# Preparing batch 2 of a linear-attention and token-mixer kernel earlier: phi of q and its transpose one block sooner, kv to mm1 four to five slots sooner, two relus on VectorE

## The chip, the cores and the metric

The kernel runs on one core of a Trainium2 chip. The metric is the device time of one execution in microseconds (us), lower is better. Times of one kernel are given as the median of several runs. Traces come from the hardware profiler; times inside a trace count from the start of its span, which is some 1.8 us shorter than the device time. In the profile lines PE is TensorE, PEld its weight loads, DVE VectorE, ACT ScalarE, POOL GpSimd and SP SyncE; L169 is line 169 of the kernel. PSUM is the memory into which TensorE writes; the granted clock is the share of full speed that TensorE was given.

## The reference

Eight batches of 576 tokens. A linear attention with eight heads of 64 feeds a mixer layer that mixes first over tokens (through 256) and then over channels (512 to 1536 and back).

```python
def phi(x):
    return np.where(x > 0, x, np.exp(x) - 1.0) + 1.0
q_p, k_p = phi(q), phi(k)
kv  = np.einsum('bhsd,bhse->bhde', k_p, v)
z   = np.sum(k_p, axis=2)
num = np.einsum('bhsd,bhde->bhse', q_p, kv)
den = np.einsum('bhsd,bhd->bhs', q_p, z)[..., None] + 1e-06
x   = (num / den)                      # heads side by side: (batch, 576, 512)
h   = np.maximum(x.T @ w_tok1, 0) @ w_tok2        # per batch
u   = x + h.T
out = u + np.maximum(u @ w_ch1, 0) @ w_ch2
```

## The kernel before

The schedule is written by hand. Each batch has a front part (phi, `kv`, `nd` = num/den, `mm1` and `mm2` over tokens) and a heavy part (`mm3` and `mm4` over channels). A block runs the heavy part of one batch as a list `big` of pieces, and after piece number s it emits whatever `fill` holds for slot s: the front part of the next batch and the loads of a later one. Each engine takes its instructions in the order in which they were emitted, so a slot is a place in five queues at once. "mm3 number 8" is the piece mm3(1, 8), and "relu 8" the relu behind it.

```python
def phi_exp(nm, n, j0, nj):            # ScalarE
    nc.scalar.activation(out=e, in_=f, func=AF.Exp)
def phi_add(nm, n, j0, nj):            # VectorE
    nc.vector.tensor_scalar(out=y, in0=f, scalar1=1.0, ..., op0=ALU.add)
def phi_end(nm, n, j0, nj):            # VectorE: max(min(e, 1), y)
    nc.vector.tensor_scalar(out=e, in0=e, scalar1=1.0, ..., op0=ALU.min)
    nc.vector.tensor_tensor(out=dst..., in0=e..., in1=y..., op=ALU.max)
def phi(nm, n, c):
    phi_exp(nm, n, 2*c, 2); phi_add(nm, n, 2*c, 2); phi_end(nm, n, 2*c, 2)

def vcast(n, c, copy=nc.scalar.copy):  # v to bf16; half 0 on ScalarE, half 1 on VectorE
    ...
def qtr_dma(n):                        # transpose of phi(q), two DMAs from SyncE's queue
    for a in range(2):
        nc.sync.dma_start_transpose(out=qT[n % 2]..., in_=qp[half[a]]...)

def nd(n, g, rs):                      # 2 or 4 matmuls, then VectorE: den, 1/den, x = num/den
    nd_mm(n, g, rs); nd_end(n, g, rs)
def mm1(n):                            # 10 matmuls; number 5 and 10 need the x of nd20 and nd21
    ...                                # then two relus on ScalarE into ar

def mm3(n, mc, kjs=range(NDM), dve=False):     # 4 matmuls into one of four PSUM buffers
    ...
    if dve: nc.vector.tensor_scalar(out=cr..., in0=ps, scalar1=0.0, ..., op0=ALU.max)
    else:   nc.scalar.activation(out=cr..., in_=ps, func=AF.Relu)

# block 0 (batch 0's mm3 and mm4, with the front part of batch 1), cut
big = [... 12 x mm3(0, mc) ..., 12 x m4_0(kc)]
at0 = {"kv": 14, "nd00": 15, ..., "nd20": 19, "nd21": 20, "mm1": 21}
fill += [(23, fn) for fn in (mm4_end(0, 0), mm4_end(0, 1), mm2_half(1, 0), ...)]
# block 1 (batch 1's mm3, tails, mm4, with the front part of batch 2)
big = [mm3(1, mc, second halves) for mc in 0, 1, 2] + m3(1, 3) + m3t + m4(0, [4, 5, 6, 7, 8])
at1 = {"kv": 11, "nd00": 13, ..., "nd21": 18, "mm1": 20, "mm2a": 21, "mm2b": 22, "mm2t": 24, ...}
fill = phi("q", 2, 0 / 1) at 0, 2; qtr_dma(2) and load_all(3) at 3; phi("k", 2, 0 / 1) at 4, 6;
       vcast(2, 0) at 8, vcast(2, 1, VectorE) at 9; phi("q", 3) at 19, 23; ...
```

Of the kernel before, what the change touches and what calls it, by code (L numbers as in the profile page):

```python
# [18 lines left out]
def kernel(  # L19
# [20 lines left out]
    nc = tc.nc  # L40
# [13 lines left out]
    NCH = DCH // 128  # L54
# [54 lines left out]
    def load(nm, n, c, gate=None):  # L109
        src_ = src[nm][n].rearrange("(j a) (p t) d -> (a p) j (t d)", a=2, t=T)  # L110
        js = slice(2 * c, 2 * c + 2)
        return after(nc.sync.dma_start(out=raw[nm, n % 2][:, js], in_=src_[:, js]), gate)
# [9 lines left out]
    def phi_exp(nm, n, j0, nj):  # L122
        f = raw[nm, n % 2][:, j0:j0 + nj].rearrange("p j f -> p (j f)")
        e = work.tile([128, 2 * TD], BF16, name="e", tag="e", bufs=4)[:, :nj * TD]
        nc.scalar.activation(out=e, in_=f, func=AF.Exp)  # L125
        live["e", j0] = e

    def phi_add(nm, n, j0, nj):
        f = raw[nm, n % 2][:, j0:j0 + nj].rearrange("p j f -> p (j f)")
        y = work.tile([128, 2 * TD], BF16, name="y", tag="y", bufs=1)[:, :nj * TD]  # L130
        nc.vector.tensor_scalar(out=y, in0=f, scalar1=1.0, scalar2=None, op0=ALU.add)  # L131
        for j in range(nj):
            live["y", j0 + j] = y[:, j * TD:]

    def phi_end(nm, n, j0, nj):
        c, i = divmod(j0, 2)
        dst = (kp if nm == "k" else qp)[:, c, :, i:i + nj]
        e, y = live["e", j0], live["y", j0][:, :nj * TD]
        nc.vector.tensor_scalar(out=e, in0=e, scalar1=1.0, scalar2=None, op0=ALU.min)  # L139
        nc.vector.tensor_tensor(  # L140
            out=dst.transpose([0, 2, 1, 3]), in0=e.rearrange("p (i t d) -> p i t d", i=nj, t=T),
            in1=y.rearrange("p (i t d) -> p i t d", i=nj, t=T), op=ALU.max)

    def phi(nm, n, c):
        phi_exp(nm, n, 2 * c, 2)
        phi_add(nm, n, 2 * c, 2)
        phi_end(nm, n, 2 * c, 2)

    def vcast(n, c, copy=nc.scalar.copy):
        js = slice(2 * c, 2 * c + 2)  # L150
        copy(out=vs[:, js, :, 0:D],  # L151
             in_=raw["v", n % 2][:, js].rearrange("p j (t d) -> p j t d", t=T))
# [9 lines left out]
    def kv(n, cs):  # L162
        b = n % 2
        ps = ps_sm.tile([128, 2, 512], FP32, name="kv_ps", tag="sm")[:, :, 0:2 * D1].rearrange(
            "p a (c e) -> p a c e", c=2)
        for c in cs:
            for t in range(T):
                for a, i in QUARTERS:
                    nc.tensor.matmul(out=ps[half[i], a, c], lhsT=kp[half[a], c, t, i],  # L169
                                     rhs=vs[half[a], 2 * c + i, t],  # L170
                                     start=(t == 0), stop=(t == T - 1))
        cs = slice(cs[0], cs[-1] + 1)
        for i in range(2):
            at = slice(i * D1, (i + 1) * D1)
            nc.scalar.copy(out=kvbd[b][half[i], cs, :, at].transpose([0, 2, 1, 3]),
                           in_=ps[half[i], :, cs])
# [13 lines left out]
    def qtr(n, c, put=nc.scalar.copy):  # L190
        tp = ps_sm.tile([128, 2, 8, 128], BF16, name="tp", tag="sm")
        for h, ts in enumerate(TS):
            qtr_mm(c, ts, tp[:, h])
        for h, ts in enumerate(TS):
            qtr_put(n, c, ts, tp[:, h], put)

    def qtr_dma(n):
        for a in range(2):
            nc.sync.dma_start_transpose(
                out=qT[n % 2][:, 2 * TD * a:2 * TD * (a + 1)].rearrange("p (f s) -> p f s", s=D),  # L200
                in_=qp[half[a]].rearrange("p c t i d -> p (c t i d)"))
# [26 lines left out]
    def nd(n, g, rs):  # L228
        nd_mm(n, g, rs)
        nd_end(n, g, rs)  # L230
# [215 lines left out]
    def w2_put(kt):  # L446
        nc.scalar.copy(out=w2p[:, TD * kt:TD * (kt + 1)].rearrange("k (t p) -> k t p", t=T),
                       in_=w2r[:, kt].transpose([0, 2, 1]))
# [8 lines left out]
    def utr_dma(n, rs):  # L457
        b = n % 2
        nc.sync.dma_start_transpose(
            out=uT[b][:, rs[0]:rs[0] + len(rs)].rearrange("p r j c -> p (r j) c"),  # L460
            in_=u[b][:, rs[0]:rs[0] + len(rs)].rearrange("p r d -> p (r d)"))
# [7 lines left out]
    def mm3(n, mc, kjs=range(NDM), dve=False):  # L469
        b = n % 2  # L470
        if kjs[0] == 0:
            part_of[mc] = ps_big.tile([128, 512], FP32, name="c_ps", tag="big")
        ps = part_of[mc]
        for kj in kjs:
            nc.tensor.matmul(out=ps, lhsT=wc1[:, kj, 128 * mc:128 * mc + 128],  # L475
                             rhs=uT[b][:, :, kj],
                             start=(kj == 0), stop=(kj == NDM - 1))
        if kjs[-1] == NDM - 1 and dve:
            nc.vector.tensor_scalar(out=cr[b][:, mc, :], in0=ps, scalar1=0.0, scalar2=None,
                                    op0=ALU.max)  # L480
        elif kjs[-1] == NDM - 1:
            nc.scalar.activation(out=cr[b][:, mc, :], in_=ps, func=AF.Relu)  # L482
# [49 lines left out]
    def prep_k(n, g, copy=nc.scalar.copy):  # L532
        phi("k", n, g)
        vcast(n, g, copy)

    def load_all(n, nms):
        if n < B:
            for nm in nms:
                for g in range(2):
                    load(nm, n, g)  # L540
# [51 lines left out]
    dve, act = nc.vector.tensor_copy, nc.scalar.copy  # L592
# [57 lines left out]
    def steps(n):  # L650

        out_ = [("kv", lambda: kv(n, range(2)))]
        if n == 1:
            puts = [nc.scalar.copy, nc.vector.tensor_copy if n == 1 else nc.scalar.copy]
            out_ += [(f"qt{c}", lambda c=c: qtr(n, c, puts[c])) for c in range(2)]
        for i, rs in enumerate(([0, 1], [2, 3], [4])):
            for g in range(2):
                out_.append((f"nd{i}{g}", lambda g=g, rs=rs: nd(n, g, rs)))
        out_.append(("mm1", lambda: mm1(n)))
        if n > 1:  # L660
            out_ += [("mm2a", lambda: mm2(n, [0, 1])), ("mm2b", lambda: mm2(n, [2, 3])),
                     ("mm2t", lambda: mm2(n, [R]))]
            out_ += [("uta", lambda: utr_dma(n, [0, 1])), ("utb", lambda: utr_dma(n, [2, 3]))]
            if n % 2:
                out_.append(("utt", lambda: utr_tail_dma(n // 2)))
        return out_

    def run(bigs, fill):
# [5 lines left out]
        for s, fn in fill:  # L674
            assert s < len(bigs)

    m3 = lambda n, k0=0: [lambda mc=mc: mm3(n, mc) for mc in range(k0, NCH)]
    m3t = [lambda i=i: mm3_tail(i) for i in range(3)]
    m4 = lambda p, ts: [lambda t=t, i=i: mm4(p, t, range(4 * i, 4 * i + 4))
                        for t in ts for i in range(3)]  # L680
# [6 lines left out]
    big = [lambda mc=mc: mm3(0, mc, range(2, 4)) for mc in range(3)] + \  # L687
# [4 lines left out]
    fill = [(2, mm2_first_tail)]  # L692
# [4 lines left out]
                 (en, lambda nm=nm, c=c: phi_end(nm, 1, 2 * c, 2))]  # L697
    late = [("vc", lambda: vcast(1, 0)), ("vc", lambda: vcast(1, 1, nc.vector.tensor_copy))]
    fill += [(16 + kt, lambda kt=kt: w2_put(kt)) for kt in range(NT)]
    first = steps(1)  # L700
    for nm, fn in first[1:3] + late + first[0:1] + first[3:]:
        fill += [(at0[nm], fn)]
# [7 lines left out]
    for mc in range(3):  # L710
        mm3(1, mc, range(0, 2))
    utr_tail(0)
    big = [lambda mc=mc: mm3(1, mc, range(2, 4)) for mc in range(3)] + m3(1, 3) + m3t + m4(0, [4, 5, 6, 7, 8])
    at1 = {"kv": 11, "nd00": 13, "nd01": 14, "nd10": 15, "nd11": 16, "nd20": 17, "nd21": 18,
           "mm1": 20, "mm2a": 21, "mm2b": 22, "mm2t": 24, "uta": 21, "utb": 22}
    fill = [(s, lambda g=g: phi("q", 2, g)) for g, s in ((0, 0), (1, 2))]
    fill += [(3, lambda: qtr_dma(2)), (3, lambda: load_all(3, "qkv"))]
    fill += [(s, lambda g=g: phi("k", 2, g)) for g, s in ((0, 4), (1, 6))]
    fill += [(8, lambda: vcast(2, 0)), (9, lambda: vcast(2, 1, nc.vector.tensor_copy))]
    fill += [(at1[nm], fn) for nm, fn in steps(2)]  # L720
    fill += [(s, lambda g=g: phi("q", 3, g)) for g, s in ((0, 19), (1, 23))]
    fill += [(24, lambda: qtr_dma(3)), (24, lambda: load_all(4, "qkv"))]
    fill += [(s, lambda g=g: prep_k(3, g)) for g, s in ((0, 25), (1, 27))]
    run(big, sorted(fill, key=lambda e: e[0]))

    AT3 = {"kv": 1, "nd00": 3, "nd01": 4, "nd10": 5, "nd11": 6, "nd20": 7, "nd21": 8,
# [3 lines left out]
    for n in range(2, B):  # L730
        p, b = divmod(n, 2)
        if b == 0:
            big = m3(n) + m4(p, [0, 1, 2, 3])
        else:
            big = m3(n) + m3t + m4(p, [4, 5, 6, 7, 8] if n + 1 < B else [8, 4, 5, 6, 7])
        fill = []
# [40 lines left out]
```

## Time and profile before

| | before |
|---|---|
| time, median of 3 runs | 268.45 us (267.95 to 268.59) |
| span of the profiled run | 266.5 us |
| TensorE / VectorE / ScalarE busy | 96% / 59% / 50% |

The prediction below shows the page's first part, the stretch of mm3 in block 1 and the end of block 0. The timeline of TensorE of the kernel before, later in block 1 and at the start of block 2 (start, duration, engine, line, operation, tiles, count):

```profile
79.88 1.28 PE L261 MATMUL h_ps<-ar,w2p 128*128 128x512 bf16 x4
81.00 1.02 PE L501 MATMUL h_ps<-wc,cr 128*128 128x512 bf16 x4
81.86 1.03 PE L261 MATMUL h_ps<-ar,w2p 128*128 128x512 bf16 x4
...
91.02 1.07 PE L169 MATMUL kv_ps<-vs,kp 64*64 64x65 bf16 x72
```

Four such matmuls without a hole are recorded with 1.03 us; the first group has 1.28. That is how a short hole shows: no idle time is listed, the group is only longer. And the list of what TensorE waited for, in the kernel before (total, times, longest):

```profile
PE kv_ps L169 <- ACT vs L151: 0.5, 1, 0.5
...
PE nd_ps L210 <- DMA qT<-qp: 0.3, 1, 0.3
```

The first is batch 2's kv at 67.1 us; the second is batch 4's nd at 120.4, far behind the change.

### The profile page before, as it was taken

Reading aid. Unit: us, or ns where it says so; the run is one execution under the profiler, and the core shown is the slowest. Engines: PE = TensorE matmul, PEld = TensorE weight load, DVE = VectorE, ACT = ScalarE, POOL = GpSimd, SP = SyncE. Lnnn points to the kernel's source line nnn. Section 1 sums busy time; section 2 is a strip of 40 time slices with the busy share of each in tenths; the row PEclk is TensorE's granted clock in tenths of the full one; section 3 lists DMA queues with packets and bytes.
Section 4 is the critical chain, followed back from the end, with each engine's and each line's share of the span. In section 5 each row is a group of like instructions: output and inputs, shape, how many; then the busy total and the mean of one; then the engine's idle time right before and its main releaser. Section 6 shows DMA issues by size and latency. Waiting matters only on the chain.

```text
span 266.5 us, 5141 instructions
## 1 busy us (share of the span) xinstructions
PE 256.1 (96%) x2107; PEld 133.9 (50%) x2107; DVE 157.4 (59%) x309; ACT 132.9 (50%) x202; POOL 32.6 (12%) x54
## 2 busy tenths in 40 slices
PE   7899989999999999999999999999999999999992
PEld 3684445553744454445564554445564554444641
DVE  5864967469587876947684296938684272420121
ACT  5735764269718368525771358425870353036300
POOL 9710200110000300030001300030001300000000
PEclk9999999999999999999999999999999999999999
DMA  7999999353957695799999990671066500730043
GB/s 259 248 203 282 367 197 398 138 132 97 345 200 156 151 387 204 87 210 373 323 410 225 287 391 9 143 164 41 2 130 120 118 2 0 157 99 2 0 118 79
DMA packets 49927, 48.34 MB, mean 181 GB/s; under 512 B 30256, under 2 KB 35248, under 8 KB 49904
## 3 DMA queue, kind: packets, MB, share of 16 engines
q1 hardware_dynamic: 41824, 35.53, 45.1%
q0 software_dynamic: 7440, 11.44, 20.3%
q10 hardware_dynamic: 640, 1.05, 1.2%
q8 instruction: 16, 0.26, 0.4%
q14 instruction: 7, 0.06, 0.1%
HBM read 35.85 MB, written 9.44 MB: 170 GB/s over the span
## 4 chain that ended last, share of the span: by engine, by line
PE 78%; DVE 7%; DMA 5%; ACT 4%; issue 2%; POOL 1%; ACTq 0%; POOLq 0%
PE h_ps L501 31%; PE c_ps L475 23%; PE a_ps L248 6%; PE h_ps L261 5%; PE c_ps L489 4%; PE nd_ps L210 3%; DMA qT<-qp 3%; DMA cr<-in_v_dram 3%; DVE y L131 2%; PE kv_ps L169 1%; ACT cr L482 1%; ACT e L125 1%; DVE e L139 1%; DVE kp L140 1%; PE bank L363 1%
## 5 line engine op out<-in xcount | busy, mean ns | idle before, releaser
L475 PE MATMUL c_ps<-uT,wc 128*128 128x512 bf16 x384 | 91.3, 379 | 0.7 <-ACT uT L444 0.4
L482 ACT ACTIVATE cr<-c_ps 128x512 bf16<-128x512 f32 x93 | 54.4, 603 | 74.6 <-PE c_ps L475 74.4
L501 PE MATMUL h_ps<-wc,cr 128*128 128x512 bf16 x384 | 87.9, 379 | 0.0
L501 PEld LDWEIGHTS <-cr 128*128 128x128 bf16 x384 | 37.0, 98 | 42.1
L475 PEld LDWEIGHTS <-wc 128*128 128x128 bf16 x384 | 35.9, 98 | 37.7 <-issue 1.8
L518 DVE TENSOR_TENSOR o_sb<-h_ps,u 128x512 f32<-128x512 f32 x32 | 21.8, 688 | 27.3 <-PE h_ps L501 27.2
L523 POOL DMA_DIRECT2D out_dram<-o_sb x24 | 14.4, 606 | 155.1 <-DVE o_sb L518 155.1
L222 DVE TENSOR_TENSOR x<-nd_ps,den 128x512 bf16<-128x512 f32 (+1 forms) x42 | 25.3, 602 | 1.5
L139 DVE TENSOR_SCALAR e<-e 128x1152 bf16<-128x1152 bf16 x30 | 13.9, 463 | 12.4 <-ACT e L125 12.3
L125 ACT ACTIVATE e<-k_raw 128x1152 bf16<-128x1152 f32 x16 | 18.8, 1174 | 2.3 <-DMA k_raw<-in_k_dram 2.3
L273 DVE TENSOR_TENSOR u<-h_ps,x 128x1024 bf16<-128x1024 f32 x12 | 14.3, 1219 | 8.8 <-PE h_ps L261 8.8
L125 ACT ACTIVATE e<-q_raw 128x1152 bf16<-128x1152 f32 x16 | 18.6, 1162 | 1.1 <-DMA q_raw<-in_q_dram 1.1
L219 DVE TENSOR_SCALAR den<-nd_ps 128x8 f32<-128x8 f32 (+1 forms) x42 | 6.8, 163 | 19.7 <-PE nd_ps L210 19.2
L251 ACT ACTIVATE ar<-a_ps 128x512 bf16<-128x512 f32 x14 | 7.6, 595 | 18.1 <-PE a_ps L248 18.1
L210 PEld LDWEIGHTS <-qT 128*128 128x128 bf16 x140 | 11.4, 98 | 10.0 <-DMA qT<-qp 0.6
L261 PE MATMUL h_ps<-ar,w2p 128*128 128x512 bf16 x60 | 16.0, 379 | 0.1
L210 PE MATMUL nd_ps<-kvbd,qT 128*128 128x130 bf16 x140 | 15.3, 223 | 0.3 <-DMA qT<-qp 0.3
L248 PE MATMUL a_ps<-x,w 128*128 128x512 bf16 x56 | 14.4, 379 | 0.0
L151 ACT CAST vs<-v_raw 128x1152 bf16<-128x1152 f32 x12 | 14.0, 1163 | 0.0
L528 DVE TENSOR_TENSOR o_sb<-h_ps,ut 128x512 f32<-128x512 f32 x4 | 2.8, 690 | 18.7 <-PE h_ps L501 18.7
L131 DVE TENSOR_SCALAR y<-q_raw 128x1152 bf16<-128x1152 f32 x16 | 12.4, 775 | 0.3
L140 DVE TENSOR_TENSOR qp<-e,y 128x1152 bf16<-128x1152 bf16 x16 | 12.1, 759 | 0.6
(102 smaller groups left out, 215.4 us busy)
## 6 DMA issues: line engine op xcount, KB each, us to landing
k_raw<-in_k_dram SPq DMA_DIRECT2D x16, 576.0 KB, 8.6
q_raw<-in_q_dram SPq DMA_DIRECT2D x16, 576.0 KB, 7.2
v_raw<-in_v_dram SPq DMA_DIRECT2D x14, 576.0 KB, 10.4
out_dram<-o_sb POOLq DMA_DIRECT2D x24, 256.0 KB, 3.8
wc<-in_moe_w_ch_dram POOLq DMA_DIRECT2D x8, 384.0 KB, 9.8
out_dram<-o_sb SPq DMA_DIRECT2D x10, 128.0 KB, 2.3
out_dram<-o_sb ACTq DMA_DIRECT2D x8, 128.0 KB, 2.6
out_dram<-o_sb POOLq DMA_DIRECT2D x6, 128.0 KB, 7.3
```

What stands on the lines that cost most here:

```text
L125: nc.scalar.activation(out=e, in_=f, func=AF.Exp)
L131: nc.vector.tensor_scalar(out=y, in0=f, scalar1=1.0, scalar2=None, op0=ALU.add)
L139: nc.vector.tensor_scalar(out=e, in0=e, scalar1=1.0, scalar2=None, op0=ALU.min)
L140: nc.vector.tensor_tensor(out=dst.transpose([0, 2, 1, 3]), in0=e.rearrange("p (i t d) -> p i t d", i=nj, t=T), in1=y.rearrange("p (i t d) ...
L210: nc.tensor.matmul(out=o[:, a], lhsT=qT[b][:, t0:t0 + 128], rhs=kvbd[b][:, c, a], start=True, stop=True)
L222: nc.vector.tensor_tensor(out=x[b][:, rs[0]:rs[0] + m, HG * D * g:HG * D * (g + 1)].rearrange("p r (h d) -> p r h d", h=HG), in0=v_[:, :, ...
L248: nc.tensor.matmul(out=ps[:, mt], lhsT=w1t[:, b, ms] if r == R else w1[:, r, ms], rhs=x[b][:, r, :], start=(r == 0), stop=(r == R))
L261: nc.tensor.matmul(out=ps[:, i], lhsT=w2v(kt, r, b), rhs=ar[b][:, kt, :], start=(kt == 0), stop=(kt == NT - 1 and not add))
L475: nc.tensor.matmul(out=ps, lhsT=wc1[:, kj, 128 * mc:128 * mc + 128], rhs=uT[b][:, :, kj], start=(kj == 0), stop=(kj == NDM - 1))
L482: nc.scalar.activation(out=cr[b][:, mc, :], in_=ps, func=AF.Relu)
L501: nc.tensor.matmul(out=ps, lhsT=crt[:, kc, :] if t == 8 else cr[b][:, kc, 128 * r:128 * r + 128], rhs=wc2[:, kc, :], start=(kc == 0), stop ...
L518: nc.vector.tensor_tensor(out=o, in0=ps, in1=u[b][:, r, :], op=ALU.add)
```

## The change

The intent: in block 1, ScalarE does twelve relus, four exps and a cast of batch 2 while TensorE does mm3, and falls behind. So the phi of batch 2's q, its transpose and the next loads go to the end of block 0, where ScalarE idles; the rest of batch 2's front part moves four or five slots up; two relus go to VectorE; and the preparation of batch 3 moves one or two slots up.

```diff
@@ block 0 @@
+    fill += [(20 + g, lambda g=g: phi("q", 2, g)) for g in range(2)]
+    fill += [(22, lambda: qtr_dma(2)), (22, lambda: load_all(3, "qkv"))]
@@ block 1 (lines shortened) @@
-    big = [...] + m3(1, 3) + m3t + m4(0, [4, 5, 6, 7, 8])
-    at1 = {"kv": 11, "nd00": 13, ... "nd21": 18, "mm1": 20, "mm2a": 21, "mm2b": 22, "mm2t": 24, "uta": 21, "utb": 22}
-    fill = [(s, lambda g=g: phi("q", 2, g)) for g, s in ((0, 0), (1, 2))]
-    fill += [(3, lambda: qtr_dma(2)), (3, lambda: load_all(3, "qkv"))]
-    fill += [(s, lambda g=g: phi("k", 2, g)) for g, s in ((0, 4), (1, 6))]
-    fill += [(8, lambda: vcast(2, 0)), (9, lambda: vcast(2, 1, nc.vector.tensor_copy))]
+    big = [...] + [lambda mc=mc: mm3(1, mc, dve=mc in (4, 7)) for mc in range(3, NCH)] + m3t + m4(0, [4, 5, 6, 7, 8])
+    at1 = {"kv": 7, "nd00": 8, ... "nd21": 13, "mm1": 15, "mm2a": 17, "mm2b": 18, "mm2t": 20, "uta": 17, "utb": 18}
+    fill = [(s, lambda g=g: phi("k", 2, g)) for g, s in ((0, 0), (1, 2))]
+    fill += [(4, lambda: vcast(2, 0)), (5, lambda: vcast(2, 1, nc.vector.tensor_copy))]
-    phi("q", 3) at 19, 23; qtr_dma(3), load_all(4) at 24; prep_k(3) at 25, 27
+    phi("q", 3) at 19, 21; qtr_dma(3), load_all(4) at 22; prep_k(3) at 24, 26
```

More of the change, by code (lines that the diff above doesn't have):

```diff
@@ L712 @@
     utr_tail(0)
-    big = [lambda mc=mc: mm3(1, mc, range(2, 4)) for mc in range(3)] + m3(1, 3) + m3t + m4(0, [4, 5, 6, 7, 8])
-    at1 = {"kv": 11, "nd00": 13, "nd01": 14, "nd10": 15, "nd11": 16, "nd20": 17, "nd21": 18,
-           "mm1": 20, "mm2a": 21, "mm2b": 22, "mm2t": 24, "uta": 21, "utb": 22}
-    fill = [(s, lambda g=g: phi("q", 2, g)) for g, s in ((0, 0), (1, 2))]
-    fill += [(3, lambda: qtr_dma(2)), (3, lambda: load_all(3, "qkv"))]
-    fill += [(s, lambda g=g: phi("k", 2, g)) for g, s in ((0, 4), (1, 6))]
-    fill += [(8, lambda: vcast(2, 0)), (9, lambda: vcast(2, 1, nc.vector.tensor_copy))]
+    big = [lambda mc=mc: mm3(1, mc, range(2, 4)) for mc in range(3)] + [lambda mc=mc: mm3(1, mc, dve=mc in (4, 7)) for mc in range(3, NCH)] + m3t + m4(0, [4, 5, 6, 7, 8])
+    at1 = {"kv": 7, "nd00": 8, "nd01": 9, "nd10": 10, "nd11": 11, "nd20": 12, "nd21": 13,
+           "mm1": 15, "mm2a": 17, "mm2b": 18, "mm2t": 20, "uta": 17, "utb": 18}
+    fill = [(s, lambda g=g: phi("k", 2, g)) for g, s in ((0, 0), (1, 2))]
+    fill += [(4, lambda: vcast(2, 0)), (5, lambda: vcast(2, 1, nc.vector.tensor_copy))]
     fill += [(at1[nm], fn) for nm, fn in steps(2)]
-    fill += [(s, lambda g=g: phi("q", 3, g)) for g, s in ((0, 19), (1, 23))]
-    fill += [(24, lambda: qtr_dma(3)), (24, lambda: load_all(4, "qkv"))]
-    fill += [(s, lambda g=g: prep_k(3, g)) for g, s in ((0, 25), (1, 27))]
+    fill += [(s, lambda g=g: phi("q", 3, g)) for g, s in ((0, 19), (1, 21))]
+    fill += [(22, lambda: qtr_dma(3)), (22, lambda: load_all(4, "qkv"))]
+    fill += [(s, lambda g=g: prep_k(3, g)) for g, s in ((0, 24), (1, 26))]
     run(big, sorted(fill, key=lambda e: e[0]))
```

## The prediction

> **What bounds the kernel now.** I read the page's first part, then the timeline of TensorE, then those of ScalarE and VectorE around each hole in it. The first part of the page:
>
> ```profile
> PE 256.1 (96%) x2107; PEld 133.9 (50%) x2107; DVE 157.4 (59%) x309; ACT 132.9 (50%) x202; POOL 32.6 (12%) x54
> PEclk9999999999999999999999999999999999999999
> ```
>
> TensorE is busy 256.1 of 266.5 us at the full clock; the others have room. The change neither adds nor removes a matmul, so it can win or lose only holes in TensorE's stream. The busy figure hides part of them: a 128x512 matmul is recorded with 379 ns, while four back to back take 0.86 us on the chain of waits, 0.216 each. So I look for starts more than 0.216 us apart. In the stretch that the change touches (46 to 92 us) they lie in batch 1's mm3, whose relus share ScalarE with the preparation of batch 2. The timeline there, all engines (start, duration, engine, line, operation, count, idle time before and its releaser):
>
> ```profile
> 56.62 9.97 PE L475 MATMUL c_ps<-uT,wc 128*128 128x512 bf16 x42
> 57.31 0.60 ACT L482 ACTIVATE cr<-c_ps 128x512 bf16<-128x512 f32 x1
> 57.80 1.17 ACT L125 ACTIVATE e<-q_raw 128x1152 bf16<-128x1152 f32 x1
> 58.85 1.09 ACT L482 ACTIVATE cr<-c_ps 128x512 bf16<-128x512 f32 x2
> 59.80 1.18 ACT L125 ACTIVATE e<-q_raw 128x1152 bf16<-128x1152 f32 x1
> 60.85 1.10 ACT L482 ACTIVATE cr<-c_ps 128x512 bf16<-128x512 f32 x2
> 61.51 0.76 DVE L140 TENSOR_TENSOR qp<-e,y 128x1152 bf16<-128x1152 bf16 x1
> ...
> 65.82 1.23 ACT L151 CAST vs<-v_raw 128x1152 bf16<-128x1152 f32 x1
> 66.24 0.76 DVE L151 CAST vs<-v_raw 128x1152 bf16<-128x1152 f32 x1
> ...
> 67.11 0.77 PE L169 MATMUL kv_ps<-vs,kp 64*64 64x65 bf16 x72 [0.51 <-ACT vs L151]
> ```
>
> ScalarE has no idle note from 57.31 on: relu, exp, two relus, exp, and so on. From 56.62 to kv's first matmul at 67.11 there are 10.49 us for 42 matmuls, which need 42 x 0.216 = 9.07. Entering kv costs 0.09 everywhere (116.52 to 117.47 us for four matmuls in the next block), so **1.33 us are stalls**: 0.15, 0.30 and 0.30 where a PSUM buffer (four of them) is still with a late relu, and 0.58 where kv waits for the cast of v. Two more lie later: four mm2 matmuls at 79.88 recorded with 1.28 instead of 1.03 us (0.26, the second half of `ar` not yet out), and batch 3's kv at 91.02 with 1.07 instead of 0.77 (0.29, for kp). The whole prize is 1.33 + 0.26 + 0.29 = 1.9 us, 0.7%.
>
> **What the Trainium skill says.** "Perfetto Trace Analysis", Identifying the Most-Contended Engine: matmul occupancy is no good measure of headroom. The trace agrees (379 ns recorded, 216 apart). "TensorE: Matmul & The Clock Gate", Step-by-step: matmuls stay in program order, only weight loads are pulled ahead. The trace agrees: while kv stands at 66.5 to 67.1, the ready mm3_tail behind it does not run. "PSUM — Partial Sum Buffer", Engine vs sequencer instructions: the queues of ScalarE and VectorE are strict FIFO. It agrees: at 57.2 VectorE idles 1.8 us for one exp. "VectorE: DVE Perf Modes", The perf-mode tier table: PSUM operands keep an operation from the fast modes. It agrees in direction: 463 ns for 128x1152 of SBUF, 675 ns for the smaller 128x512 relu from PSUM.
>
> **The change part by part.**
>
> *1. phi of q of batch 2 goes into batch 0's block (slots 20, 21).* Data: q's two halves are issued at 37.25 and 37.7 us and the trace gives 6.0 and 6.8 us to landing: 43.25 and 44.5. ScalarE is free then:
>
> ```profile
> 49.21 1.08 ACT L251 ACTIVATE ar<-a_ps 128x512 bf16<-128x512 f32 x2 [6.35 <-PE a_ps L248]
> ```
>
> so two exps of 1.17 run at about 43.3 and 44.5 for nothing. VectorE is the trouble. The order of its instructions in the changed program is: nd20's three, the first phi's three, nd21's three, the second phi's three, o_sb. Before:
>
> ```profile
> 45.67 0.42 DVE L222 TENSOR_TENSOR x<-nd_ps,den 128x256 bf16<-128x256 f32 x1
> 46.19 0.16 DVE L219 TENSOR_SCALAR den<-nd_ps 128x4 f32<-128x4 f32 x1
> 46.39 0.18 DVE L221 RECIPROCAL den<-den 128x4 f32<-128x4 f32 x1
> 46.60 0.42 DVE L222 TENSOR_TENSOR x<-nd_ps,den 128x256 bf16<-128x256 f32 x1
> 50.29 1.29 DVE L518 TENSOR_TENSOR o_sb<-h_ps,u 128x512 f32<-128x512 f32 x2 [3.27 <-PE h_ps L501]
> ```
>
> and on TensorE:
>
> ```profile
> 46.85 1.03 PE L248 MATMUL a_ps<-x,w 128*128 128x512 bf16 x4
> 47.72 0.38 PE L248 MATMUL a_ps<-x,w1t 128*128 128x512 bf16 x1
> ```
>
> mm1's fifth matmul, at 47.72, needs nd21's x, ready at 47.02. One phi between others takes 1.83 us from its start to the next one's (76.49 to 78.32). With it at 46.01, nd21's den starts at 47.84, its x at 48.25, done 48.67, and the fifth matmul goes at about 48.73: **+1.0 us**, and mm1 and all behind it shift. The second phi runs 48.6 to 50.4 beside mm1 and ends before o_sb's new time (51.3): free. A hole of 3.27 us was there for both, but the first was put ahead of the instruction that TensorE waits for.
>
> *2. Transpose and loads of batch 3 sooner.* The two transposes (some 4 us each to land) start about 50.5 instead of 62.4; nothing waited for them before. Worth 0.
>
> *3. Block 1 without the q work; kv at slot 7, two relus on VectorE.* Times as before, without the 1.0. ScalarE: relu0 57.31, exp k 57.80, relu1 58.85, relu2 59.35, exp k 59.80, relu3 60.85, v cast 61.35 to 62.55. The sequence up to relu3 is unchanged, so mm3 number 7 still waits 0.15 for its buffer, and the last matmul before kv goes at 62.17. VectorE: the k phis sit where the q phis sat, the second ends at 62.27; then relu4 (0.67), then its v cast 62.95 to 63.7. kv needs ScalarE's cast (62.55, 0.14 late) and, for its second half, VectorE's (63.7, when TensorE would be there at about 62.9): mm3 number 8 starts near 64.18 where 63.03 would be free: stalls 1.15. nd00 follows one slot after kv instead of two, and the kvbd copies (0.76) end at 65.08: 0.1 more. Together 1.25 against 1.33: **-0.1**. The relus after that keep up (ScalarE's five exps and casts in this stretch became three).
>
> *4. Later slots.* mm2a now comes two slots after mm1 instead of one: -0.26. The k phis of batch 3 start a slot sooner and VectorE, back to back from 82.9 to 92 us before, has the q phi behind it sooner: -0.29.
>
> Sum: +1.0 - 0.1 - 0.26 - 0.29 = +0.35, so 268.45 + 0.35 = **268.8 us**.
>
> **The rivals.** *It works as meant*: the early phi costs nothing and kv stops waiting: -1.9, 266.5 us. For it: the holes are real, ScalarE's load falls. Against it: the strict order on VectorE twice, at nd21 and at the cast behind relu4. If nd21's wait alone fails to appear: 267.8. *Late data*: q lands under about 400 GB/s of traffic; e is needed at 46.7 and its exp ends at 44.5, so 2.2 us of slack; landing 3 us late would add about 1 us: 269.8, and ScalarE's relu of mm1 would sit behind the exps. *Collisions*: batch 3's loads run with the output stores instead of after them; both were hidden, and batch 4's transpose (0.3 us of waiting at 120.4) may move either way: +-0.3. In none does another engine become the bound.
>
> **Range and chances.** Three runs before spread over 0.6 us; the hand schedule may be off by 0.5 at each of two places; hence 267.8 to 269.7. Being faster by 2% needs 5.4 us, nearly three times all the holes there are; being slower by 2% needs five such waits as I found.
>
> **What would show it.** In the changed profile: (1) a hole of about 1 us inside mm1 of batch 1 near 48 us, released by VectorE's x; without it I am 1 us too high. (2) kv of batch 2 split by a wait of about 0.7 us for the cast of v on VectorE. (3) the four mm2 matmuls at 1.03 us and batch 3's kv at 0.77. (4) the q transposes issued near 50 us with no waiter. I'd be wrong most if the q data land late, or if a new hole opens after 92 us.

## The result and the profile after

| | before | after |
|---|---|---|
| time, median of 4 runs each | 268.40 us (267.95 to 268.59) | 268.61 us (268.28 to 269.13) |
| span of the profiled run | 266.5 us | 266.8 us |
| granted clock, profiled run | 1.0 | 0.998 |

The ratio after to before is 1.0012, with a 95% interval of 0.9991 to 1.0032: the same. Ratios here are the mean time of one kernel's runs over the mean of the other's runs of the same rounds, so they are not quite the ratio of the medians. Executions over 1.5% slower than the fastest of the same kernel are left out of the means.

The end of block 0 in the changed kernel, timeline of VectorE, ScalarE and TensorE (as above; in brackets the idle time before, and what ended it):

```profile
43.18 2.25 ACT L125 ACTIVATE e<-q_raw 128x1152 bf16<-128x1152 f32 x2
...
46.41 0.75 DVE L131 TENSOR_SCALAR y<-q_raw 128x1152 bf16<-128x1152 f32 x1
...
47.26 0.81 PE L248 MATMUL a_ps<-x,w 128*128 128x512 bf16 x3
47.57 0.76 DVE L140 TENSOR_TENSOR qp<-e,y 128x1152 bf16<-128x1152 bf16 x1
48.25 0.15 DVE L219 TENSOR_SCALAR den<-nd_ps 128x4 f32<-128x4 f32 x1
...
48.65 0.42 DVE L222 TENSOR_TENSOR x<-nd_ps,den 128x256 bf16<-128x256 f32 x1
...
49.13 0.38 PE L248 MATMUL a_ps<-x,w1t 128*128 128x512 bf16 x1 [1.06 <-DVE x L222]
```

The exps are done long before they are needed. One whole phi (46.41 to 48.25, 1.84 us) stands before nd21's den, and mm1's fifth matmul, due at 48.12 us (0.86 us behind the first, at 47.26), runs at 49.13: a hole of 1.01 us. (The trace lacks the record of the fourth, so the list shows 1.06.)

Block 1, the same view:

```profile
62.92 0.76 DVE L140 TENSOR_TENSOR kp<-e,y 128x1152 bf16<-128x1152 bf16 x1
63.59 0.68 DVE L479 TENSOR_SCALAR cr<-c_ps 128x512 bf16<-128x512 f32 x1
...
63.97 0.48 PE L169 MATMUL kv_ps<-vs,kp 64*64 64x65 bf16 x36
64.20 0.75 DVE L151 CAST vs<-v_raw 128x1152 bf16<-128x1152 f32 x1
...
65.00 0.48 PE L169 MATMUL kv_ps<-vs,kp 64*64 64x65 bf16 x36 [0.54 <-DVE vs L151]
```

kv's 72 matmuls are cut in two: the second half waits for VectorE's cast of v, which stands behind relu 4 (line 479). Later, mm2's first matmuls, batch 3's kv and batch 4's first nd:

```profile
77.55 1.03 PE L261 MATMUL h_ps<-ar,w2p 128*128 128x512 bf16 x4
...
91.89 0.78 PE L169 MATMUL kv_ps<-vs,kp 64*64 64x65 bf16 x72
...
120.50 0.54 PE L210 MATMUL nd_ps<-kvbd,qT 128*128 128x130 bf16 x4
```

And the list of TensorE's waits:

```profile
PE a_ps L248 <- DVE x L222: 1.1, 1, 1.1
PE kv_ps L169 <- DVE vs L151: 0.8, 2, 0.5
```

kv's wait for ScalarE has become one for VectorE, a new wait of 1.1 us is there, and batch 4's wait for qT has left the list. It is not quite gone: the four nd matmuls at 120.50 are recorded with 0.54 us where others have 0.40, so 0.14 of its 0.44 us remain.

**A ledger of the trace.** Every run's code is the same up to 40 us, and yet batch 1's kv started anywhere between 38.36 and 39.08 us in the thirteen profiles. To keep this out, I set the start of that kv as zero in each trace and list how far a run is behind (+) or ahead (-) of the kernel before at later landmarks on TensorE:

| us against before | batch 1's tail transposes (before: 56.4) | kv of batch 3 (91.0) | kv of batch 4 (117.5) | kv of batch 5 (150.2) and the end |
|---|---|---|---|---|
| after | +1.01 | +0.47 | +0.18 | -0.01 |

So block 0 lost 1.01, block 1 won 0.54 (1.01 to 0.47), batch 3's kv 0.29, and a further 0.19 came in block 3. Net nothing, with one trace of each; the timed runs say +0.1%, with zero inside the interval.

### The profile page after: what moved, and what is told of

It reads as the page before. It is cut to its first block, busy times and chain, and to the rows that moved or that the text cites. A ratio compares the mean times of both kernels' runs of the same rounds, so it can differ in the third digit from the quotient of the medians.

```text
span 266.8 us, 5122 instructions
## 1 busy us (share of the span) xinstructions
PE 255.8 (96%) x2088; PEld 134.1 (50%) x2107; DVE 158.2 (59%) x311; ACT 132.6 (50%) x200; POOL 33.4 (13%) x54
## 4 chain that ended last, share of the span: by engine, by line
PE 89%; DVE 6%; ACT 2%; issue 1%; POOL 0%; POOLq 0%; ACTq 0%
PE h_ps L501 33%; PE c_ps L475 29%; PE a_ps L248 5%; PE h_ps L261 5%; PE c_ps L489 4%; PE bank L545 3%; PE nd_ps L210 3%; PE kv_ps L169 2%; DVE x L222 1%; ACT e L125 1%; PE bank L363 1%; PE bank L413 1%; DVE y L131 1%; DVE vs L151 1%; PE bank L385 1%
## 5 line engine op out<-in xcount | busy, mean ns | idle before, releaser
L482 ACT ACTIVATE cr<-c_ps 128x512 bf16<-128x512 f32 x91 | 53.5, 598 | 79.0 <-PE c_ps L475 78.9
L501 PE MATMUL h_ps<-wc,cr 128*128 128x512 bf16 x376 | 86.9, 379 | 0.5
```

Of the source, the lines that this page charges most:

```text
L482: nc.scalar.activation(out=cr[b][:, mc, :], in_=ps, func=AF.Relu)
L501: nc.tensor.matmul(out=ps, lhsT=crt[:, kc, :] if t == 8 else cr[b][:, kc, 128 * r:128 * r + 128], rhs=wc2[:, kc, :], start=(kc == 0), stop ...
```

## The experiments

My theory: the changed kernel's time is the sum of a hole made by the order of VectorE's queue at nd21 (+1.0), a hole moved from ScalarE's cast of v to VectorE's, and two mended later holes. Rivals: it is the price of doing q early at all (ScalarE, late data); or the engines are full in this stretch and no order helps. All experiments gave correct results. Each was timed in three or five rounds beside the kernel before. Below, a kernel is called faster or slower only where the interval excludes 1. "Ledger" is the last column of the table above: the trace's end against the kernel before, from batch 1's kv on.

### Both phis ahead of nd21

```diff
-    fill += [(20 + g, lambda g=g: phi("q", 2, g)) for g in range(2)]
+    fill += [(20, lambda g=g: phi("q", 2, g)) for g in range(2)]
```

> The suspected cost doubled: both phis of q ahead of nd21 on VectorE. My theory: mm1's hole grows by one phi, 1.83 us, from 1.0 to 2.85 us, and nothing takes it back: 270.4 us. Rival (the hole is not VectorE's order but the arrival of q or ScalarE): it stays at 1.0, 268.6.

Measured: 271.83 us, ratio 1.0119 (1.0092 to 1.0146); ledger +2.0. The timeline of TensorE:

```profile
51.12 0.38 PE L248 MATMUL a_ps<-x,w1t 128*128 128x512 bf16 x1 [3.01 <-DVE x L222]
```

The wait grows from 1.06 to 3.01 us, by 1.95: one more phi (two in a row are 1.94 apart, start to start, in this trace). The size of the hole is set by what stands ahead of nd21. The median is 3.2 us above the changed kernel's where the profiled spans differ by 2.1 (268.9 to 266.8); the profiled run was the fastest of its six (270.68). The clock may explain that further 1 us of the other five: four of them have a mean granted clock of 0.990 to 0.996, the profiled run 0.999, and two traces further down show slow matmuls behind a long hole. No trace of those five is kept, so it isn't shown.

### Both phis behind nd21, a slot later

```diff
-    fill += [(20 + g, lambda g=g: phi("q", 2, g)) for g in range(2)]
+    fill += [(21 + g, lambda g=g: phi("q", 2, g)) for g in range(2)]
```

> The changed kernel with both early phis of q one slot later, so that VectorE's program has nd21's three instructions ahead of the first phi. My theory (the 1 us hole in mm1 of batch 1 is nd21's x standing behind a 1.83 us phi on VectorE): the hole goes, x is ready as in the kernel before, the two phis fill VectorE's 3.27 us hole and delay the first o_sb by some 0.3 us, which mm2_half hides. 267.6 us, 0.8 to 1.0 below the changed kernel. Rival (the hole is the price of putting ScalarE's exps or q's late data there, whatever the order): the hole stays or moves to mm2_half, 268.4 or more.

Measured: 268.74 us, ratio 1.0012 (0.9989 to 1.0036); ledger +0.5. My number missed. The hole in mm1 is gone, as the theory says, but the timeline shows another one in mm2_half:

```profile
50.82 1.17 ACT L125 ACTIVATE e<-q_raw 128x1152 bf16<-128x1152 f32 x1
...
52.02 0.46 DVE L139 TENSOR_SCALAR e<-e 128x1152 bf16<-128x1152 bf16 x1 [1.74 <-ACT e L125]
...
54.36 0.60 PE L288 MATMUL h_ps<-ar,w2p 128*128 128x256 bf16 x4 [0.67 <-ACT u L291]
```

My edit was careless: at slot 22 the second exp is emitted after mm1's two relus, and ScalarE takes it only when those have waited for mm1. VectorE then stands 1.74 us for it, and its o_sb and u come late. The hole in mm2_half has a second part that I had not thought of: PSUM buffers are assigned when the kernel is built, and in the compiled order of this build the matmul at 54.36 waits for ScalarE, where in the kernel before and in the changed kernel the same one waits for VectorE. So it got another buffer, one that ScalarE frees only at 54.31. The rival is not refuted by this run.

### Exps early, VectorE's part behind nd21

```diff
-    fill += [(20 + g, lambda g=g: phi("q", 2, g)) for g in range(2)]
+    fill += [(20, lambda g=g: phi_exp("q", 2, 2 * g, 2)) for g in range(2)]
+    for g in range(2):
+        fill += [(21, lambda g=g: phi_add("q", 2, 2 * g, 2)), (21, lambda g=g: phi_end("q", 2, 2 * g, 2))]
```

> A repaired version of the run with the phis behind: that run put the second exp of q behind mm1's two relus on ScalarE's queue, so VectorE stood 1.74 us for it and the hole moved into mm2_half. Here both exps stay at slot 20 (ScalarE, idle there), and only VectorE's six instructions go behind nd21's three. Everything else is the changed kernel. My theory: mm1's hole (1.06) goes and none comes in mm2_half, since the two phis end at about the time of the first o_sb; stalls in the trace between 46 and 57 us fall by 0.9 to 1.0, and the time is 0.9 below the changed kernel: about 267.6. Rival (the phis just don't fit into VectorE's 3.27 us hole): 0.5 us or more of new waits in mm2_half, at most 0.5 gained.

Measured: 267.70 us, ratio 0.9978 (0.9949 to 1.0007; one of six runs at 269.52); ledger at the tail transposes 0.00 instead of +1.01, at the end -1.3. Neither mm1 nor mm2_half has a hole that the kernel before doesn't have. So q can be prepared at the end of block 0 for nothing; only the order of VectorE's queue costs 1.0 us. The rival falls. (That rests on the trace: the timed interval still includes 1. 0.45 of the 1.3 come only after 117.5 us, 0.44 of it from batch 4's wait for qT, which this profile lacks.)

### The first part of the change alone

Block 0 as in the changed kernel; block 1's slots and relus as before, less the q work.

```diff
-    (block 1 of the changed kernel)
+    big = ... + m3(1, 3) + m3t + m4(0, [4, 5, 6, 7, 8]); "kv": 11, "nd00": 13, ... as before
+    fill = [(s, lambda g=g: phi("k", 2, g)) for g, s in ((0, 4), (1, 6))]   # no phi of q, no qtr_dma(2), no load_all(3)
```

> Only the first part of the change: phi of q, its transpose and the loads in batch 0's block; block 1 as in the kernel before (kv at 11, all relus on ScalarE). My theory: +1.0 for nd21's x, and -1.3 because ScalarE, without the two exps of q, keeps up with the relus and kv no longer waits; the waits of mm2a (0.26) and of batch 3's kv (0.29) stay. About 268.1 us, 0.3 below the kernel before. Rival (it is kv at slot 7 and the two relus on VectorE that mend block 1): block 1's stalls stay, 269.4.

Measured: 268.23 us, ratio 0.9989 (0.9965 to 1.0013); ledger +1.00 at the tail transposes, -0.32 at batch 3's kv, -0.5 at the end. The timeline of TensorE in block 1:

```profile
58.13 9.23 PE L475 MATMUL c_ps<-uT,wc 128*128 128x512 bf16 x42
67.29 0.78 PE L169 MATMUL kv_ps<-vs,kp 64*64 64x65 bf16 x72
```

42 matmuls in 9.23 us are 42 x 0.216 and the last one's tail (379 ns recorded, 0.216 apart: 0.16): **no stall at all**, against 1.33 us before. Taking the phi of q out of block 1 (two exps off ScalarE, six instructions off VectorE) mends it completely. That kv moved to slot 7 and that two relus moved to VectorE had no part in it; with them, 1.03 us of stalls came back (0.15 for a PSUM buffer, 0.82 before and in kv, 0.06 at nd00).

### The two relus back on ScalarE

```diff
-    ... [lambda mc=mc: mm3(1, mc, dve=mc in (4, 7)) for mc in range(3, NCH)] + m3t ...
+    ... m3(1, 3) + m3t ...
```

> The changed kernel with the two relus of batch 1 back on ScalarE. My theory: they are worth nothing where they stand, for relu4 delays VectorE's cast of v by 0.67 us just before kv needs it. Without it, kv's second half no longer waits (0.54), but ScalarE's cast comes 0.5 later behind relu4 and nd00 waits some 0.4 for kvbd: within 0.3 us of the changed kernel, 268.6. Rival (the relus are what relieves ScalarE and saves kv): 0.6 us or more worse, 269.3.

Measured: 268.45 us, ratio 1.0001 (0.9978 to 1.0025); ledger -0.1, as the changed kernel within 0.1. kv is whole again, but starts 0.59 us late for ScalarE's cast, and nd00 comes 0.50 late for kvbd (by starts; the list shows 0.51 and 0.32). The relus on VectorE are worth nothing where they stand.

### VectorE's cast of v ahead of relu 4

```diff
-    fill += [(4, lambda: vcast(2, 0)), (5, lambda: vcast(2, 1, nc.vector.tensor_copy))]
+    fill += [(4, lambda: vcast(2, 0)), (3, lambda: vcast(2, 1, nc.vector.tensor_copy))]
```

> The changed kernel with VectorE's cast of v ahead of relu4 instead of behind it. My theory: kv's second half then waits no longer than for its cast, which ends 0.67 sooner; relu4 ends later and holds mm3 number 8's PSUM buffer a little: stalls between 57 and 67 us 0.3 to 0.5 less than in the changed kernel, 268.2. Rival (the k phi on VectorE, not relu4, is what kv waits for): no change, 268.6.

Measured: 267.76 us, ratio 0.9973 (0.9946 to 1.0000); ledger -0.7, as against -0.0 of the changed kernel. kv is whole (72 matmuls in 0.92 us, 0.14 above the others), and mm3 number 8 behind it waits for nothing: in the compiled order of this build its PSUM buffer is one that ScalarE frees, where in the changed kernel it has relu 4's. At batch 3's kv the trace is 0.60 us ahead of the changed kernel's, above the 0.3 to 0.5 that I expected. It was relu 4 that kept kv.

### kv one slot later, on top of the careless edit

```diff
+    (both phis behind nd21, a slot later)
-    at1 = {"kv": 7, "nd00": 8, ... "mm1": 15, "mm2a": 17, "mm2b": 18, "mm2t": 20, "uta": 17, "utb": 18}
+    at1 = {"kv": 8, "nd00": 10, ... "mm1": 17, "mm2a": 19, "mm2b": 20, "mm2t": 22, "uta": 19, "utb": 20}
```

> As the run with the phis behind nd21, and in block 1 kv of batch 2 at slot 8 instead of 7, nd00 two slots after it, mm1 at 17, mm2 at 19, 20 and 22. My theory (kv at slot 7 stands 0.7 us for VectorE's cast of v behind relu4): the cast is out when kv comes, the split of kv goes, 0.8 us less than with the phis behind alone: 266.8 us, about 0.6% under the kernel before. Rival (VectorE and ScalarE are simply full in this stretch, and the wait moves to nd00 or to a PSUM buffer): no gain over the run with the phis behind, 267.6.

Measured: 268.39 us, ratio 0.9998 (0.9972 to 1.0023); ledger -0.0. A miss. kv is no longer cut, but mm3 number 8 now comes first and waits 0.54 us for its PSUM buffer, which relu 4 still holds: on VectorE it runs only at 63.66 us, behind the phi of k. The wait moved to a PSUM buffer, as the rival said. Against the run it builds on, the trace wins 0.34 us by batch 3's kv (ledger +0.62 to +0.28) where I expected 0.8: the place of kv mends a part, the order in the cast-first run 0.60.

### Both orders on VectorE mended

The changed kernel with the edits "exps early" and "cast ahead of relu 4", and nothing else.

> The changed kernel with both of its orders on VectorE mended and nothing else: the early exps as in that run (nd21 ahead of the phis), and the cast of v ahead of relu4. From batch 1's kv to the end, the first alone took 1.25 us off the changed kernel's trace and the second 0.67. If the changed kernel's loss is these two waits, they add up: 1.9 us under the changed kernel, 266.6 us, ratio to the kernel before 0.993. If they hide one another or the saved time comes back as a wait for a transpose, as in the run with both holes: 267.5 or more.

Measured: 266.53 us (265.95 to 267.07), ratio **0.9930** (0.9906 to 0.9955); ledger -1.9. The sum comes out to within 0.1: -1.3 and -0.7. The timeline around kv and mm1:

```profile
46.97 0.75 DVE L131 TENSOR_SCALAR y<-q_raw 128x1152 bf16<-128x1152 f32 x1
...
47.74 0.38 PE L248 MATMUL a_ps<-x,w1t 128*128 128x512 bf16 x1
...
62.22 0.76 DVE L151 CAST vs<-v_raw 128x1152 bf16<-128x1152 f32 x1
...
62.59 0.91 PE L169 MATMUL kv_ps<-vs,kp 64*64 64x65 bf16 x72
62.88 1.28 DVE L479 TENSOR_SCALAR cr<-c_ps 128x512 bf16<-128x512 f32 x2
```

This is the kernel with the lowest median, 1.8 us or 0.7% under the kernel before, and its interval excludes 1.

### All holes by the other way, and what then came in the way

I also built a version on the kernel before's block 1: exps early, kv at 11, all relus on ScalarE, mm2 two slots behind mm1, and the phis of batch 3 early.

```diff
+    (block 0 as in "exps early"; block 1 as in "the first part alone", with)
+    "mm1": 20, "mm2a": 22, "mm2b": 23, "mm2t": 25, "uta": 22, "utb": 23
+    phi("q", 3) at 19, 21; qtr_dma(3), load_all(4) at 24; prep_k(3) at 24, 26
```

> The version that the readings point to: block 0 as in the run with the exps early; block 1 with kv at slot 11 and all relus on ScalarE, as before (the run with the first part alone showed that kv's waits go once the two exps of q are away); mm2 of batch 2 two slots after mm1 and the phis of batch 3 at the changed kernel's slots. My theory: the 1.33, 0.26 and 0.29 us of the kernel before are all gone and the 1.06 of the changed kernel never comes: 1.8 us below the kernel before, 266.6 us, ratio 0.993. Rival (moving kv sooner is what pays): no better than the run with the exps early alone, 267.6.

Measured: 267.77 us (265.51 to 270.28), ratio 0.9957 (0.9917 to 0.9997); six times spread over 4.8 us. Its profiled run was the slowest, so I use it only to see where time can go. Its fastest run is below all six of the kernel with both orders mended (lowest 265.95). Why the six scatter stays open: the clock alone isn't it, for the one at 269.07 us had a mean of 1.000. Ledger: -1.57 at batch 3's kv, as the theory says, then +1.95 at batch 4's: here is a wait for batch 3's q that no other profile has. TensorE's waits, and, in the view of the tile qT, the time from issue to landing of batch 3's two transposes:

```profile
PE nd_ps L210 <- DMA qT<-qp: 2.0, 1, 2.0
```

```profile
DMA to landing us min/median/max: 3.8/5.4/7.0
```

The wait is not all. Behind it TensorE runs slowly; in the view by stretches (bounds, length, TensorE busy, granted clock, share and GB/s of the DMA engines):

```profile
94.20:96.30 2.10, 2.10 (x11) 0.59 1.03 400
```

It is 0.56 in the next 1.9 us and 1.00 again from 98.2. From the first of batch 3's nd groups to the third the trace needs 6.0 us (92.00 to 98.01) where the kernel before needs 2.2 (93.76 to 95.95): 2.1 for the wait and some 1.7 for the clock. In the kernel before the two transposes took 3.6 and 3.7 us, though its loads of batch 4 were also issued right behind them. Two runs looked into it. First, the transpose of q ahead of those of u:

```diff
-    phi("q", 3) at 19, 21; qtr_dma(3), load_all(4) at 24
+    phi("q", 3) at 19, 19; qtr_dma(3) at 20, load_all(4) at 26
```

> The run with both holes mended, which moved TensorE 1.6 us sooner by batch 3's kv and then stood 2.0 us in its profiled run for the transpose of batch 3's q (issued 85.65 us, behind the two transposes of u, its second half landing 7.0 us after its issue beside the loads of batch 4), and whose six times spread over 4.8 us. Here both phis of batch 3's q stand at slot 19, the transpose of q is issued ahead of those of u, and the loads of batch 4 four slots after both. My theory: the wait for qT in block 2 is gone, the times draw together again, and the 1.8 us show: 266.4 us, ratio 0.992 to 0.994. Rival (the spread and the loss are of something else than that transpose, say the chip's clock): no change, 267.8 with a spread of several us.

Measured: 271.45 us, ratio 1.0117 (1.0086 to 1.0148); ledger +3.4. I was wrong: nd no longer waits for qT, but mm3 of batch 2 waits for the transposes of u, which now come behind. TensorE's waits, and its timeline behind the wait:

```profile
PE c_ps L475 <- DMA uT<-u: 3.7, 1, 3.7
```

```profile
92.16 3.39 PE L475 MATMUL c_ps<-uT,wc 128*128 128x512 bf16 x8 [3.65 <-DMA uT<-u]
```

Again the wait is not all: the eight matmuls behind it are recorded with 3.39 us instead of 1.89, at a granted clock of 0.55 (92.1 to 95.4 us). That is another 1.5 us. Behind the holes of 1.1 us (the changed kernel, the next run) and behind the 3.0 us of the profiled run with both phis ahead the clock stayed at 1.00, so when it falls isn't settled here.

(The later slot of the loads meant nothing: SyncE's queue has nothing else to wait for and issued them at 88.32 us, as soon as it was free.) Second, the loads held back by a semaphore until the transpose has landed:

```diff
-    fill += [(24, lambda: qtr_dma(3)), (24, lambda: load_all(4, "qkv"))]
+    fill += [(24, lambda: qtr_dma(3)), (24, lambda: load_all(4, "qkv", live["qT"]))]   # first load waits for the last transpose
```

> The run with both holes mended, whose transpose of batch 3's q landed 7.0 us after its issue beside the loads of batch 4, and one edit: those loads wait until that transpose has landed. Theory A (the loads, 1.7 MB issued right behind, stretch the transpose's second half from under 4 to 7 us): the landing comes back to 4 us, the wait for qT at block 2's start goes, and the time is 266.0 to 266.6 us with a spread under 1.5 us. Theory B (the transposes are late because the two of u and the two of q follow one another on one queue, whatever else runs): the wait for qT stays at 1 to 2 us, 267.5 us or more.

Measured: 267.13 us (265.87 to 267.62), ratio 0.9938 (0.9908 to 0.9968); ledger -1.57 at batch 3's kv and -1.85 at batch 4's, then -1.00. The time misses the 266.0 to 266.6 that I expected. The landing view of batch 3's transposes:

```profile
DMA to landing us min/median/max: 3.7/4.2/4.7
```

With the loads away the slower half lands in 4.7 us instead of 7.0 and the wait is gone, as theory A has it; but there is one trace of each, and that of the run without the gate is a slow one. That the gate makes the kernel faster isn't shown: the intervals of the two ratios overlap. (The loads are six of 576 KB, 3.4 MB, not the 1.7 that I wrote.) Since the same loads did no harm in the kernel before, they are not all of it: there the output stores were issued at 89.89 us, after the second transpose was well under way, and in the run without the gate at 87.61, half a us behind its issue. How much is due to which stays open. But the loads came later, and in block 3 batch 4's nd waits 1.1 us for its own transpose: part of the gain is given back. The spread narrows to 1.75 us, not to the 1.5 that I expected.

## Why the prediction was right

It said 268.8 us, in a range of 267.8 to 269.7; 268.61 was measured. Term by term, from the trace:

| term of the sum | predicted | measured | shown by |
|---|---|---|---|
| nd21's x behind a phi on VectorE | +1.0 | +1.01 | the order experiments: listed 1.06 with one phi ahead, 3.01 with two, none with none |
| block 1's mm3 to nd00 | -0.1 | -0.30 | stalls of 1.03 instead of 1.33 |
| mm2a two slots behind mm1 | -0.26 | -0.26 | no start more than 0.216 us late there |
| batch 3's kv | -0.29 | -0.29 | 0.78 us for 72 matmuls instead of 1.07 |
| transposes later on | 0 | -0.19 | batch 4's wait for qT fell from 0.44 to 0.14, and 0.12 came for batch 3's tail transpose |
| sum | +0.35 | -0.03 (ledger: -0.01) | timed runs: +0.3 (1.0012), interval -0.2 to +0.9 us |

The mechanism of each step held, and two sizes were off. **Block 1**: I gave the phi's last instruction and relu 4 their recorded 0.76 and 0.67 us, but they hold VectorE's queue for only 0.67 and 0.61 (62.92 to 63.59 to 64.20), and the kvbd copies kept nd00 by 0.06 instead of 0.1. That is 0.19 of the 0.22 by which 1.25 was too high. **Later transposes**: I had put them in the range (0.3 either way) and not in the sum. In the kernel before, batch 4's nd loses 0.44 us, where the list of waits says 0.3, so the stake was larger than the list let me think. That the change itself shortens that wait is not shown: it is gone in every later profile but that of the run with gated loads, and there is one profile of each kernel.

**How close the number came is partly luck.** Both sizes were off in the same direction, so by the trace the sum should have been -0.03 and not +0.35; the timed median came out 0.2 us above the kernel before's, with zero inside the interval. A forecast of no change would have come as close. What the runs confirm is the terms, not their sum.

**What the count left out.** mm2_half has two holes of 0.39 us by starts (52.23 and 53.72, listed with 0.24 each, for ScalarE's copy of u). They are in the changed kernel as well, so no term changes, but the 1.9 us were the prize of this change and not all that the stretch from 46 to 92 us holds.

The rival "works as meant", 266.5 us, was the right size for what the change could bring, and refuted for the change as it is: with both orders mended it measures 266.53. "Late data" did not occur: both exps ran from 43.18 us. "Collisions" is the one that came true in small, and in large in the run with all holes by the other way.

Of what the prediction said would show: the hole in mm1 released by VectorE's x is there at 49.13; kv is cut: from its first matmul to the one behind it are 1.45 us (63.97 to 65.42) where batch 4's takes 0.72; batch 3's kv takes 0.78 us; q's transposes start at 51.04 and have no waiter; and mm2's four matmuls are recorded with 1.03 us.

## What to carry to other kernels

When TensorE is busy 96% of the time, add up the holes first: their sum bounds what a change that only fills those holes can win. Here it was 0.7%, and the kernel with both orders mended won as much. Moving work into another engine's idle time is right only if it goes behind the instruction that the busy engine waits for next: emit by engine, not by function, since one call of phi put an exp on a queue where it was free and three instructions on a queue where they cost 1 us. And when compute moves sooner, look at which transfer it then meets: in one slow run a transpose that had 2 us of slack became the wait. Such a hole can cost more than its length: behind two of them, of 2.1 and 3.8 us, TensorE lost another 1.7 and 1.5 us at a granted clock of 0.55 to 0.59.

## What the Trainium skill lacked or had wrong

- "DMA: Bandwidth & Descriptors", Rules for kernel authors: it says that a transpose next to ordinary DMAs needs nothing. The results were correct in every run, so for correctness that agrees. The page has a bandwidth for transposes, but no time to landing beside loads and stores. The same transpose of batch 3's q (64 partitions x 2304 bf16, 288 KB) landed 3.6 to 7.0 us after its issue, depending on what moved beside it, and the 128 KB transpose of batch 3's tail, with loads ahead of and behind it, 9.1 to 12.0 us.
- "Perfetto Trace Analysis", Tensor Engine Instruction: it says that a matmul's end is estimated, but not what follows for holes. Of 1.33 us of stalls in block 1 only 0.51 was listed as idle time; a 128x512 matmul is recorded with 379 ns at a pace of 216, so a hole behind one shows 0.16 us too short, and one under 0.16 doesn't show. (Where a record is missing, as before 49.13, a hole shows too long by the pace.)
- No page that I read spells out the consequence of in-order queues that cost 1 us here: a ready instruction placed ahead of a needed one is a wait. It was listed with 1.06 us behind one phi, 3.01 behind two.
- No page that I read gives the spread of a kernel's start: with the same instructions up to 40 us, one landmark came at 38.36 to 39.08 us in thirteen profiles, as large as most effects.
